# Output weights and input loads moved ahead on the DMA queues, and half-depth matmuls joined in bursts, in a fused convolution and mixing kernel

## The chip, the cores and the metric

One Trainium2 chip, one core. The metric is device time in microseconds (us), as the median of several executions. Names of the engines: PE is TensorE (matmul), PEld its weight load, DVE VectorE, ACT ScalarE, POOL GpSimd, SP SyncE. DMA has one queue for each of three kinds of traffic here: inputs are read by POOL's queue (q0 of the profile), outputs stored by SP's queue (q1), and q8 brings PE its instructions, which will matter.

Executions of a one-core kernel can be labelled slow only by their time (over 1.5% above the fastest of the same kernel). Where I meet that label below I say what was behind it, since here it was never the whole clock of a run.

## The reference, cut to what matters

```python
B, S, D = 8, 4224, 192                      # x, float32
# 1. causal depthwise convolution, 7 taps, softmaxed weights, 8 groups of 24 channels
out[b, s] = sum_k softmax(weight)[h, k] * x_pad[b, s + k]
# 2. linear attention form on that result
wq, wk = x @ w_q, x @ w_k                   # 192 -> 64
W_tok  = einsum('bsd,btd->bst', wq, wk) / sqrt(64)
mixed  = einsum('bst,btd->bsd', W_tok, x)
return maximum(mixed, 0) @ w_out            # 192 -> 192
```

The kernel never builds the 4224x4224 product: it forms G = x^T x per batch, M = w_k^T G, and then mixed = (x w_q) M.

## The kernel before: the parts that matter here

PE runs a fixed list of jobs, one letter each, and every engine does its work in the order that the list gives: Y (convolution as a banded matmul), G (six 64-column matmuls), Q (48 matmuls of 32x64 tiles), Z (one 512-column matmul; three of them give "mixed" for 1024 tokens, which lie in two halves of 64 rows; the first two each meet zeros in one half of the rows, the third serves both halves on a diagonal), O (output product of 512 tokens, two PSUM banks). Evacuations from PSUM go to ACT and DVE, also in order.

```python
    wload(WK[64:128, 2], wk_t, 0, DH, wl[1], 2)
    load(1, 0)                                   # loads of batch 1, all on POOL's queue
    load(1, 1)
    ...
    load(1, 2)
    ...                                          # zeros, identity
    load(1, 3)
    load(2, 0)
    wload(WO1[:, :], wo_t, 0, D, wl[2])          # the output weights
    wload(WO2S[0:64, :], wo_t, 128, D, wl[2])
    wload(WO2S[64:128, :], wo_t, 128, D, wl[2])
    z_wo2 = pool(lambda e: e.memset(WO2[:, :], 0.0))
    load(2, 1)
```

WO2 holds the last 64 rows of the output weights twice, on a diagonal of a zero-filled 128x384 tile, so that one full-depth matmul serves two blocks of tokens:

```python
            for j in range(2):                   # job O
                for h in range(2):
                    e.matmul(o[:, 192 * h : 192 * h + 192], z[:, h, cols], WO1[:, :],
                             start=h == 0, stop=False, **kw)
                last = e.matmul(o[:, 0:384], z[:, 2, cols], WO2[:, :], start=False, stop=True, **kw)
```

A store waits only for the evacuations that fill its buffer (`evs`):

```python
                st = P.dma("sp", lambda e, ...: e.dma_start(bass.AP(out_t, at, dims), src),
                           og[orr], evs)
```

The list was made with a model of the chip that also knows instruction fetch: `"fetch": (64, 256, 6.0, 3.0, 120.0)` says that PE's instructions come in blocks of 256, and that 6.0 us (3.0 after 120 us) have to lie between a block's start and the next one's.

Of the kernel before, what the change touches and what calls it, by code (L numbers as in the profile page):

```python
# [11 lines left out]


ORDER = (
    "YYDYYYDYDGDGGGYDGYYGDGTYTYDhYGhGTGDGGhGGHTGQYDGGWGTEMYMTYYYDZYZGGGTQYZGDGWGGDZZZ"
    "YOZOOGGGGhGGZTTHGYQGGGYYGYZDEZTYYZGZMGTGDTYGTYZTMGGGGOGOOGGHZQTGGYZGOYZOZZGYDZGY"
    "TGGZOZZOEYTTOGGYZGQGGYGTZDYZGHMhOGGZQYTGMTGYTTYOZOGOGZZGTZOYOOGZZOGZGDYGEQTGZZMG"
    "GhQOGZGYYTZOOGHGZYTOGGZMDYGGGYGZGYYOZGZGOZZGDGEOTZQGZMZGGTOYYOGTOZYGDYZZGGhMOGGT"
    "QHOGZGZTZOGZYOGGZZZYYZGOGYTTOTZOGZGhOEDQZGOYOGTGZTGGMYYOZOGGMZYZODGTOOGHZZGGYZOh"
    "GGGYThQGZZGZQZTOGYGEZYOOZZZOMYDGYMYGGZGTZOOTZZZGTGGTYDTGOGOGGQZZZGGOTTZTGZOQZGGO"  # L20
    "QGOGOEMZZZOMOOZZZOZZZZOOOZZZOOZZZOZOOOO"
)
# [3 lines left out]
    "x0": (5.0, 7.5, 9.0, 8.1, 10.2, 12.0, 13.1, 13.8), "band": 6.5, "wq": 14.0, "wk": 16.0,  # L26
    "wo": 26.0, "fill": 24.0,
    "dma": (377e3, 13.2, 1.6, {"x": 3.0, "o": 1.2}), "fetch": (64, 256, 6.0, 3.0, 120.0),
}
# [137 lines left out]
def bass_lightweight_conv__then__hypermixer_token_mlp_kernel(  # L167
# [8 lines left out]
    B, S, D = x.shape  # L176
# [16 lines left out]
    NZ = 3  # L193
# [76 lines left out]
    def rows(b, half, c, lo, hi, n, grp, deps):  # L270
        spent[0] += 0.45 + 0.055 * n
        at = (b * S + half * HALF + c * CW - 6 + lo) * D

        def f(e):
            return e.dma_start(  # L275
                XW[lo:hi, b % NX, half, c : c + n, :],
                bass.AP(x_t, at, [[D, hi - lo], [CW * D, n], [1, D]]),
            )

        return P.dma("pool", f, grp, deps)  # L280
# [62 lines left out]
    def wload(o, src, row0, width, grp, twice=1):  # L343
        spent[0] += 0.65
        n = o.shape[0]
        dims = [[width, n], [0, 2], [1, width]] if twice == 2 else [[width, n], [1, width]]
        P.dma("pool", lambda e: e.dma_start(o, bass.AP(src, row0 * width, dims)), grp)  # L347
# [104 lines left out]
    load(1, 0)  # L452
    load(1, 1)
    wq = [pool(lambda e: e.tensor_copy(WQ[:, :, :], WSQ[:, :, :]), [wl[0]], 0.55)]
    z_wk = pool(lambda e: e.memset(WK[:, 3:6], 0.0))
# [11 lines left out]
    load(2, 0)  # L467
    wload(WO1[:, :], wo_t, 0, D, wl[2])
    wload(WO2S[0:64, :], wo_t, 128, D, wl[2])
    wload(WO2S[64:128, :], wo_t, 128, D, wl[2])  # L470
    z_wo2 = pool(lambda e: e.memset(WO2[:, :], 0.0))
# [270 lines left out]
    def job_o(b, i, q):  # L742
# [19 lines left out]

        def make(bk):
            if rem:
                return [(OUT[:, orr, 0, 0:192], PS[:, bk, 0:192])]
            if tail:
                return [(
                    OUT[:, orr, q, :].rearrange("p (h r d) -> p r h d", h=2, r=2),
                    PS[:, bk : bk + 2, 0:384].rearrange("p r (h d) -> p r h d", h=2),
                )]  # L770
            return [(
                OUT[:, orr, :, 384 * q : 384 * q + 384].rearrange("p h (r d) -> p r h d", r=2),
                PS[:, bk : bk + 2, 0:384].rearrange("p r (h d) -> p r h d", h=2),
            )]
# [3 lines left out]
        def then():  # L778
            if not rem and q == 0 and not tail:
                return  # L780
            evs = [o for k in range(0 if not tail else q, q + 1) for o in made[("OUT", b, i, k)]]
            at = (b * S + 512 * i) * D
            if rem:
# [7 lines left out]
            for at, dims, src in parts:  # L791
                st = P.dma(
                    "sp",
                    lambda e, at=at, dims=dims, src=src: e.dma_start(bass.AP(out_t, at, dims), src),
                    og[orr], evs,
                )
# [3 lines left out]
            def landed(t, st=st):  # L800
# [3 lines left out]
                               (64 * 2 * D if rem else 128 * 4 * D if tail else 128 * 8 * D) * 4,  # L804
                               landed))
            flow()
# [42 lines left out]

    SWITCH = {("F", "Q"): 0.096, ("Q", "F"): 0.115}  # L850
    FILL, SEE = 0.231, 0.055
# [8 lines left out]
    for b in range(B):  # L860
        for g in range(len(GROUPS[b])):
            x_at[id(xg[b][g])] = CLOCK["x0"][g] if b == 0 else 999.0
    RATE, at0, DELAY, LAND = CLOCK["dma"]
    queue = {"x": [], "o": []}

    def flow():
        left = {k: [[t, n / RATE, f, LAND[k]] for t, n, f in v] for k, v in queue.items()}
        t = at0
        while any(left.values()):
            busy = [v for v in left.values() if v and v[0][0] <= t]  # L870
            nxt = min([v[0][0] for v in left.values() if v and v[0][0] > t] + [1e9])
            if not busy:
                t = nxt
                continue
            dt = min(min(v[0][1] for v in busy) * len(busy), nxt - t)
            t += dt
            for v in busy:
                v[0][1] -= dt / len(busy)
                if v[0][1] < 1e-9:
                    _, _, f, late = v.pop(0)  # L880
                    f(t + late)

    def land(b, part):
        def f(t):
            x_at[id(xg[b][part])] = t - 1.5 * (b == 1)
        return f

    def put(b, part, t):
        chunks = 18 * 128 if part == 0 else 16 * 128 + 2 * (6 + LAST)
        if b == 1:  # L890
            chunks = (9, 9, 8, 8)[part] * 128 + 2 * (6 + LAST) * (part == 2)
        queue["x"].append((t + DELAY, chunks * D * 4, land(b, part)))
        flow()
# [39 lines left out]

    def pick(n):
        if n == 4:
            if hold:
                return hold[0], max(banks[k][0] for k in hold)
            bk = min(range(4), key=lambda k: max(banks[j][0] for j in range(k, k + 4)))
            return bk, max(banks[k][0] for k in range(bk, bk + 4))
        if n == 1:  # L940
            bk = min((k for k in (6, 0, 1, 2, 3, 4, 5) if k not in hold),
                     key=lambda k: banks[k][0])
            return bk, banks[bk][0]
        bk = min((k for k in (0, 2, 4, 1, 3, 5) if k not in hold and k + 1 not in hold),
                 key=lambda k: max(banks[k][0], banks[k + 1][0]))
# [47 lines left out]
    def place(job, t):  # L993
# [8 lines left out]
        if job.pe:  # L1002
# [10 lines left out]
            late, code[:] = stall(job.words, pop.start, job.pe_us)  # L1013
            pop.end = free["pe"] = pop.start + job.pe_us + late
            total[0] += late
        elif kind == "GEV":
            pop = done[("G", job.name[1], NCK - 1)]
            deps += [pop] + [done[a_] for a_ in job.after if a_[1] >= 0 and a_[0] != "G"]
        else:
            pop = None  # L1020
            deps += [done[a_] for a_ in job.after if a_[1] >= 0]
        done[job.name] = pop
        emptied = []
        for make, key, n, what in job.evacs:
            pairs = make(bk)
            waits = [pop] if job.pe else list(deps)
# [39 lines left out]
            emptied.append(ev)  # L1066
        if job.pe:
            pop.name = job.name
        for k in held:
# [4 lines left out]
        if kind == "D" and job.name[1] > 1:  # L1074
            prefetch(job.name[1] + NX - 2, job.name[2])

    place(casts[0], CLOCK["x0"][1])
    head["W"] = 1
    for c in ORDER:
        if c == "h":  # L1080
            bk = pick(4)[0]
            hold[:] = range(bk, bk + 4)
            continue
        s = {"E": "GEV", "M": "MC"}.get(c, c)
# [37 lines left out]
```

## Time and profile before

| | before |
|---|---|
| device time, median (range) | 159.91 us (159.88 to 160.38) |
| span of the profiled execution | 158.0 us |
| first output matmul | 29.75 us |
| last input load landed | 122.83 us |
| PE's end, tail after it | 151.1 us, 6.9 us |

The lines behind these are in the prediction. One row that it did not read is on the same page, under the DMA queues (packets, MB, share of the 16 engines' span): PE's instruction stream, 19 blocks of 16 KB.

```profile
q8 instruction: 19, 0.31, 0.7%
```

### The profile page before, as it was taken

The page shows a single profiled execution, that of the slowest core. Times are in us where ns is not written, and L with a number is a line of the kernel's source. Part 1 is how long each engine was busy: PE and PEld are TensorE (multiplying, and loading weights), DVE is VectorE, ACT ScalarE, POOL GpSimd, SP SyncE. Part 2 cuts the span into 40 slices and gives each one's busy share as a digit, 9 for nine tenths or more (in the row PEclk, how much of TensorE's full clock was granted, in tenths as well). Part 3 has the DMA queues.
Part 4 walks back from the last instruction along what each step waited for, and adds up shares of the span by engine and source line. Part 5 has one row for each costly group of instructions (what it writes and reads, how often), then busy time and mean ns, then how long its engine had stood idle before and what let it go on. Part 6 is the DMA issues. An engine that isn't in the chain of part 4 may idle for free.

```text
span 158.0 us, 5584 instructions
## 1 busy us (share of the span) xinstructions
PE 142.7 (90%) x2428; PEld 102.2 (65%) x2428; DVE 117.8 (75%) x235; ACT 128.7 (81%) x216; POOL 59.8 (38%) x77
## 2 busy tenths in 40 slices
PE   6997759499999999999999999999999899999920
PEld 1476547374876777777776776777766677776710
DVE  6739678558889869967979988878678798677700
ACT  5566576698989999988997989999999698799940
POOL 7999899896906273301720200202020200000000
PEclk9999999999999999999999999999999999999995
DMA  3999999999999999999999999999998946279995
GB/s 105 261 193 183 192 191 190 192 191 290 193 193 323 337 276 234 207 339 327 267 318 256 323 269 262 323 287 308 310 349 214 358 168 242 74 306 374 353 372 189
DMA packets 48441, 40.83 MB, mean 258 GB/s; under 512 B 37281, under 2 KB 40481, under 8 KB 48417
## 3 DMA queue, kind: packets, MB, share of 16 engines
q0 software_dynamic: 36384, 13.35, 70.9%
q1 hardware_dynamic: 12032, 27.14, 48.0%
q8 instruction: 19, 0.31, 0.7%
q14 instruction: 6, 0.04, 0.1%
HBM read 27.86 MB, written 25.95 MB: 341 GB/s over the span
## 4 chain that ended last, share of the span: by engine, by line
PE 45%; DMA 34%; POOL 14%; issue 2%; ACT 1%; ACTq 0%; DVE 0%; POOLq 0%; DVEq 0%
DMA xw<-in_x_dram 29%; PE ps L758 8%; PE ps L639 8%; POOL xw L275 8%; PE ps L760 8%; PE ps L715 7%; PE ps L539 7%; PE ps L609 5%; DMA wo2s<-in_moe_w_out_dram 5%; POOL wk L347 2%; POOL xw L292 1%; POOL y L954 1%; ACT y L954 1%; ACT o_sb L954 1%; POOL m_sb L457 0%
## 5 line engine op out<-in xcount | busy, mean ns | idle before, releaser
L954 ACT COPY o_sb<-ps 128x768 f32<-128x768 f32 (+1 forms) x61 | 46.6, 781 | 4.4 <-PE ps L760 3.0
L954 ACT CAST y<-ps 128x864 bf16<-128x864 f32 (+6 forms) x49 | 39.9, 836 | 6.9 <-PE ps L505 3.5
L758 PE MATMUL ps<-wo,zt 128*128 128x192 bf16 x256 | 42.2, 247 | 2.1 <-DVE wo L954 2.0
L639 PEld LDWEIGHTS ps<-y 128*128 128x128 bf16 (+1 forms) x864 | 35.5, 98 | 12.5 <-issue 2.9
L760 PE MATMUL ps<-wo,zt 128*128 128x384 bf16 x128 | 41.7, 326 | 0.0
L639 PE MATMUL ps<-y 128*128 128x64 bf16 (+1 forms) x864 | 40.1, 193 | 0.5 <-DVE y L954 0.5
L954 POOL COPY y<-y 128x1152 bf16<-128x1152 bf16 x12 | 13.8, 1147 | 63.8 <-ACT y L954 51.2
L950 DVE STREAM_TRANSPOSE yb<-y 128x576 int32<-128x576 int32 x48 | 35.2, 757 | 0.1
L958 DVE TENSOR_SCALAR zt<-ps 128x512 bf16<-128x512 f32 x46 | 30.7, 683 | 5.1 <-PE ps L715 4.7
L758 PEld LDWEIGHTS ps<-wo,zt 128*128 128x128 bf16 x256 | 26.6, 114 | 12.0 <-ACT wo L954 2.2
L275 POOL DMA_DIRECT2D xw<-in_x_dram x35 | 32.5, 940 | 2.0 <-POOL xw L434 1.1
L715 PE MATMUL ps<-qt,m_sb 128*128 128x512 bf16 x96 | 31.6, 380 | 0.0
L957 ACT ACTIVATE zt<-ps 128x512 bf16<-128x512 f32 x50 | 29.1, 611 | 0.5 <-PE ps L715 0.3
L539 PE MATMUL ps<-xw,band 128*128 128x432 bf16 x96 | 24.4, 346 | 0.9 <-DMA xw<-in_x_dram 0.9
L954 DVE CAST y<-ps 128x864 bf16<-128x864 f32 (+2 forms) x19 | 19.4, 1022 | 4.5 <-PE ps L539 3.7
L954 DVE CAST qt<-ps 128x288 bf16<-128x288 f32 (+1 forms) x30 | 11.6, 424 | 9.0 <-PE ps L609 8.9
L954 ACT CAST qt<-ps 128x576 bf16<-128x576 f32 (+1 forms) x18 | 10.8, 610 | 5.9 <-PE ps L609 5.4
L609 PE MATMUL ps<-yb,wq 32*64 32x288 bf16 x768 | 15.2, 284 | 0.0
L760 PEld LDWEIGHTS ps<-wo,zt 128*128 128x128 bf16 x128 | 14.5, 114 | 0.0
L609 PEld LDWEIGHTS ps<-yb,wq 32*64 32x64 bf16 x768 | 10.5, 102 | 2.6 <-issue 0.7
L505 PE MATMUL ps<-xw,band 128*128 128x120 bf16 (+4 forms) x96 | 9.0, 233 | 2.6 <-DMA xw<-in_x_dram 1.6
L715 PEld LDWEIGHTS ps<-qt,m_sb 128*128 128x128 bf16 x96 | 8.6, 98 | 3.6 <-issue 0.7
(74 smaller groups left out, 96.7 us busy)
## 6 DMA issues: line engine op xcount, KB each, us to landing
out_dram<-o_sb SPq DMA_DIRECT2D x31, 768.0 KB, 7.4
xw<-in_x_dram POOLq DMA_DIRECT2D x14, 432.0 KB, 17.9
xw<-in_x_dram POOLq DMA_DIRECT2D x14, 384.0 KB, 26.0
o_sb<-in_x_dram SPq DMA_DIRECT2D x2, 480.0 KB, 4.4
out_dram<-o_sb SPq DMA_DIRECT2D x16, 48.0 KB, 5.5
out_dram<-o_sb SPq DMA_DIRECT2D x2, 384.0 KB, 3.8
xw<-in_x_dram POOLq DMA_DIRECT2D x2, 240.0 KB, 6.5
xw<-in_x_dram POOLq DMA_DIRECT2D x1, 288.0 KB, 6.9
```

The costliest lines, as they stand in the source:

```text
L275: return e.dma_start(XW[lo:hi, b % NX, half, c : c + n, :], bass.AP(x_t, at, [[D, hi - lo], [CW * D, n], [1, D]]),)
L505: last = e.matmul(PS[:, bk + j // per, at : at + w], BAND[:, h, :], XW[:, b % NX, half, c0:c1, GRP * h : GRP * h + GRP], start=True, stop= ...
L539: last = e.matmul(PS[:, k + j, 0 : 48 * n].rearrange("p (c h d) -> p h c d", h=2, d=GRP), BAND[:, h, :], rhs, start=True, stop=True,)
L609: last = e.matmul(PS[64 * h : 64 * h + 64, bk + i, 0:288], WQ[r, j, :], rhs, start=j == 0, stop=j == 5, skip_group_check=True)
L639: last = e.matmul(PS[:, 7, 64 * k : 64 * k + 64], y[:, 64 * k : 64 * k + 128], y[:, 64 * k : 64 * k + 64], start=c + h + k == 0, stop=c == ...
L715: return e.matmul(PS[:, bk, :], m[:, parts[k] : parts[k] + 128], q, start=True, stop=True)
L758: e.matmul(o[:, 192 * h : 192 * h + 192], z[:, h, cols], WO1[:, :], start=h == 0, stop=False, **kw)
L760: last = e.matmul(o[:, 0:384], z[:, 2, cols], WO2[:, :], start=False, stop=True, **kw)
L950: return e.transpose(o, i)
L954: return e.copy(o, i) if eng == "act" else e.tensor_copy(o, i)
L957: return e.activation(o, i, AF.Relu)
L958: return e.tensor_scalar(o, i, 0.0, None, op0=ALU.max)
```

## The change

Its intent: let reads go ahead of stores where PE will need the data, bring the output weights early, and stop spending PE time on the zero halves of the first two Z matmuls and of the 384-column output matmul. The whole job list was made anew with it. The core of it:

```diff
+GATES = {0: 8, 3: 9, 5: 10, 10: 12, 15: 14}       # store: the half batch whose load it waits for
 ORDER = (...)                                     # new list, with thirteen "A" = a burst
 CLOCK = {
-    "wo": 26.0, ... "fetch": (64, 256, 6.0, 3.0, 120.0),
+    "wo": 20.5, ... "fetch": (64, 256, 5.5, 3.5, 120.0),

     load(1, 0)
     load(1, 1)
+    wload(WO1[:, :], wo_t, 0, D, wl[2])
+    wload(WO2S[0:64, :], wo_t, 128, D, wl[2])
+    wload(WO2S[64:128, :], wo_t, 128, D, wl[2])
...
     load(1, 3)
     load(2, 0)
-    wload(WO1[:, :], wo_t, 0, D, wl[2])
-    wload(WO2S[0:64, :], wo_t, 128, D, wl[2])
-    wload(WO2S[64:128, :], wo_t, 128, D, wl[2])
     z_wo2 = pool(lambda e: e.memset(WO2[:, :], 0.0))   # stays here
     load(2, 1)

-                    og[orr], evs,
+                    og[orr], evs + wait,
...
+        def tails(e):                             # a burst: two Z, then the third-of-rows of O
+            for h in range(2):
+                rows = slice(64 * h, 64 * h + 64)
+                e.matmul(PS[:, za[h], :], M_SB[rows, ...], QT[rows, ...], start=True, stop=True)
+            for bk, z, cols in parts:
+                for r in range(2):
+                    for h in range(2):
+                        rows = slice(64 * h, 64 * h + 64)
+                        e.matmul(PS[:, bk + h, 192 * r : 192 * r + 192], z[rows, 2, cols[r]],
+                                 WO2S[rows, :], start=r == 0, stop=False)
+        def heads(e):                             # then the full-depth matmuls of the same O
+            ...
+                        e.matmul(PS[:, bk + h, 192 * r : 192 * r + 192], z[:, h, cols[r]],
+                                 WO1[:, :], start=False, stop=r == 1)
```

The planner's parts (how it models shares of the DMA engines, how banks are picked for a burst) changed too; they only produced the list and what is fixed with it, such as which bank and which evacuating engine a job gets.

## The prediction

> **What bounds the kernel now.** I read the page first, then the PE and POOL timelines of the start, the waits, the windows, and the DMA packets summed per queue. From the page:
>
> ```profile
> span 158.0 us, 5584 instructions
> PE 142.7 (90%) x2428; PEld 102.2 (65%) x2428; DVE 117.8 (75%) x235; ACT 128.7 (81%) x216; POOL 59.8 (38%) x77
> PE   6997759499999999999999999999999899999920
> DMA  3999999999999999999999999999998946279995
> q0 software_dynamic: 36384, 13.35, 70.9%
> q1 hardware_dynamic: 12032, 27.14, 48.0%
> ```
>
> PE is ragged for eight slices (31.6 us), full up to slice 30 (120 us), dented there, full until it ends. DMA is full up to 120 us, half idle for 20 us, full at the end. So three things set the time: a start in which PE waits, a long stretch of PE work, and a DMA tail. The 31.6 us of the start hold two waits that the PE timeline names:
>
> ```profile
> 20.12 0.90 PE L505 MATMUL ps<-xw,band 128*128 128x216 bf16 x8
> 22.61 0.53 PE L505 MATMUL ps<-xw,band 128*128 128x216 bf16 x4 [1.59 <-DMA xw<-in_x_dram]
> ...
> 27.23 0.53 PE L505 MATMUL ps<-xw,band 128*128 128x216 bf16 x4
> 29.75 0.33 PE L758 MATMUL ps<-wo,zt 128*128 128x192 bf16 x2 [1.99 <-DVE wo L954]
> 29.92 0.33 PE L760 MATMUL ps<-wo,zt 128*128 128x384 bf16 x1
> ```
>
> The output weights arrive last of all that the first output job (O) needs. POOL issues them late, behind batch 2's first load:
>
> ```profile
> 18.23 1.99 POOL L275 DMA_DIRECT2D xw<-in_x_dram  x2 [0.30 <-POOL xw L434]
> 20.20 0.57 POOL L347 DMA_DIRECT2D wo<-in_moe_w_out_dram  x1
> 20.75 1.10 POOL L347 DMA_DIRECT2D wo2s<-in_moe_w_out_dram  x2
> ```
>
> The later dent is one wait for the last input load (batch 7, second half), issued near 77 us and landed 46 us later, as the chain of waits shows:
>
> ```profile
> 77.17 45.66 DMA xw<-in_x_dram
> 122.83 0.14 issue
> 122.96 0.52 PE ps L539 x2
> ```
>
> The windows for 124 to 140 us show PE full and DMA at 0.55: PE has fallen behind and DMA has nothing to send.
>
> ```profile
> 124.00:140.00 16.00, 16.00 (x331) 11.92 (x328) 13.28 (x27) 14.22 (x24) 1.15 (x1) 1.00 0.55 206
> ```
>
> **What the Trainium skill says.** "DMA: Bandwidth & Descriptors", section "Queues, rings and completion order": each DMA engine takes turns between its queues, packet by packet. The trace agrees, and the turns are uneven in bytes. I counted packets in half-microsecond steps (input bytes doubled: the cast writes bf16 of float32): input alone moves about 376 GB/s; while a 768 KB store moves, input has 76 and the store 305. A store runs 2.6 us so and starts 3.4 us after its issue; the sum stays near 376 from 8 to 120 us.
>
> "TensorE: Matmul & The Clock Gate", "Part 3: Packing small matmuls — row/col tiling": matmuls on different row groups of the array run together. The trace agrees for 32x64 tiles: a Q job's 48 matmuls of 288 columns start 0.88 us before the next job, where one after the other they would take 5.9. No 64-row tile occurs in this trace. "TensorEngine Tiling (Array Packing)", "Key Properties", says that a change of mode drains the array. Here that costs some 0.24 us per Q job: 0.09 ahead of it, 0.15 in it beyond six times 0.1225.
>
> **The change part by part.** Start-to-start times of jobs in the trace are 0.655 us for O, 0.216 for a Z matmul, 0.175 for G (six 64-column matmuls), 0.366 for two 432-column Y matmuls. Summed over the job list they make 127.1 us, and 131.0 with 16 Q switches of 0.24. Up to the first O they make 14.0, so 117.0 remain. PE took 121.35 us for these (29.75 to 151.1): 4.35 us of stalls, of which 1.03 is the wait for batch 7. So 3.3 us are ordinary stalls, and I keep them.
>
> 1. Output weights earlier. The three issues (1.67 us of POOL) move ahead of the remaining loads of batch 1, to about 12.5 us. Loads land in order at full rate: batch 1's second load landed at 19.44, so the weights should land near 20 instead of 29.1. Batch 1's third load is pushed from 22.5 to about 23.0 (0.2 MB more ahead of it). The Q weights' cast goes from 12.4 to 14.1 and the identity from 16.2 to 17.8; the first Q (16.25 before) and the transpose (19.36) still come after. The new list puts 2 us more work before that third load's use, which covers the 1.59 us wait. Walking it: batch 0's last Y at 14.3 (its data at 13.36 is unchanged), nine G and a Q to 17.1, two Y and the transpose to 18.2, a wait to 19.45 for batch 1's second load, two Y, MM, Q and five Z to 22.6, a wait to 23.0, then five matmul jobs, Y and G, to 25.3. Evacuation of those Z, Q and Y tiles (7 us of ACT and DVE together in 3.5) may cost half a microsecond: first burst at 25.8. Work ahead of it is 12.8 + 0.5 = 13.3. The lag of the clock behind the work was 29.75 - 14.0 = 15.75 and becomes 12.5: **3.2 us gained**.
>
> 2. Bursts. Thirteen times, two Z (0.43) and one O (0.655), 1.087 together, become: two half-depth Z at once (0.216), four half-depth tail matmuls in two pairs (0.17), four heads (0.33), and two switches (about 0.21 to 0.24). That is 0.93 to 0.96; **1.9 us gained** in all, half of what it would be without switches. A burst needs two Z banks and two O banks free at once, so I take off 0.4 for the set. The O job's 128x384 matmul used half of its rows and columns on zeros, and two of three Z matmuls have zeros in one half: this is why no work is lost. Evacuations stay as many and as large.
>
> 3. Gated stores. The bytes stay; their order changes. Gates hold store 0 for batch 4's first half, 3 for its second, 5, 10 and 15 for the first halves of batches 5, 6 and 7. With the measured 376, 76 and 305 GB/s I moved both queues by hand along the new list: batch 3's halves land at 38 and 42 us (used 41 and 47), batch 4's at 47 and 51, store 0 leaves at 47 instead of 32.5; batch 5's at 65 and 69 (used 70 and 81), batch 6's at 82 and 87 (92 and 97), batch 7's at 100 and 105 (105 and 116). After each gate opens, the 3.4 us before the store moves are reads alone: 1.3 MB, most of a half batch of 1.6 MB. So **1.0 us gained**, the wait at 122 us. The same walk for the kernel before gave 121.7 for its last load (measured 122.83). Eight output buffers: the job that reuses store 10's buffer comes at 93, that store lands at 90; the others have 3 us or more. No new wait on this count, but the margin is small.
>
> Sum: 3.2 + 1.9 + 1.0 - 0.4 = 5.7, so PE ends at 145.4 instead of 151.1. From PE's end to the span's end were 6.9 us (last copy, stores queued at 366 GB/s); the last job is the same kind, and the last eight stores of 4.9 MB need 13 us in both lists, with 10.5 us of work from the first of them to the last against 9.7 before. I keep 6.9. Span 152.3, plus the 1.9 us between span and measured time: 154.2.
>
> **Rivals.**
> A. *DMA is the bound.* 52.4 MB at 376 GB/s are 139 us, plus 3 at the start and 2 to land: 145. For it: DMA full up to 120 us. Against: 9 us idle between 120 and 142, so earlier work fills that hole first; the total stays 7 us under my span. If stores held back come out in a heap at the end, 156.
> B. *The gates turn on the kernel.* The 3 us margins of output buffers fail, PE waits for copies that wait for stores near 77, 93 or 110 us. Each miss costs 1 to 3 us; two of them give 157 to 158.
> C. *64-row matmuls don't overlap.* A burst is then 1.09 + 0.2 of switches + nothing saved, the thirteen cost 2.6 instead of gaining 1.9: 158.5. For it: no such tile in the trace, and each 192-column pair needs two weight loads of 128 columns in 85 ns. Against: the Q job's overlap, and full-depth weight loads already keep up with one matmul per 29 ns in G.
> D. *Evacuation is the bound.* ACT was busy 109.4 of 120.5 us in the steady part, DVE 98.1: 91 and 81%. The steady part shortens by 2% only, so ordinary stalls may grow by a microsecond or two: 155.5.
> E. *The gates are needed more than I count.* The walk with the new list but no gates loses 4 us on batch 3, as store 0 would take bandwidth at 33 us. That says nothing against the sum, but an undo of the gates alone should show it.
>
> **Range and chances.** The start is good to about 1 us, the bursts to 1, the rest (B, D) leans late. 154.2 with 152.0 to 157.2. Two per cent faster is 156.7, which needs 3.2 of the 5.7 us: 0.87. Within two per cent, by C or two misses of B: 0.11. Slower: 0.02.
>
> **What would show it.** First output matmul near 25.8 us and no wait on the output weights; landings of these near 20; a burst's start-to-start near 0.94 with two half-depth matmuls starting together; no PE wait for input after 30 us; store 0 issued near 47; DMA share in 120 to 140 us well over 0.55; PE's end near 145.4 and 7 us of tail. Wrong if output copies wait for stores, if bursts exceed 1.09, or if the tail grows past 8 us.

## The result, and the profile after

| | before | predicted | after |
|---|---|---|---|
| device time, median | 160.14 (4 runs beside it) | 154.2 | **157.83** (4 runs, 157.18 to 158.32) |
| span, profiled execution | 158.0 | 152.3 | 156.2 |
| first output matmul | 29.75 | 25.8 | 27.22 |
| from there to PE's end | 121.35 | 119.6 | 122.8 |
| PE's end, tail | 151.1, 6.9 | 145.4, 6.9 | 150.0, 6.2 |

The ratio of after to before is 0.985 (95% interval 0.981 to 0.990). Ratios here are the mean time of one kernel's fast runs over that of the other's of the same rounds, so not quite the ratio of the medians. The change gained 2.3 us, where I had said 5.7 and given 0.87 to a gain of over two per cent; with a line drawn at two per cent, these runs count as the same. The three terms of the miss add up to the 3.9 us between the spans: the start is 1.4 late, the long stretch 3.2 longer, the tail 0.7 shorter.

The page of the changed kernel, cut to the lines that answer those of before:

```profile
span 156.2 us, 5628 instructions
PE 138.2 (88%) x2431; PEld 101.4 (65%) x2456; DVE 119.7 (77%) x239; ACT 128.7 (82%) x213; POOL 58.5 (37%) x76
...
PE   6989758989999899999999999999697999998940
...
DMA  3999999999999999999999999999997556599896
...
q8 instruction: 19, 0.31, 0.7%
```

PE's work did shrink, from 142.7 us busy to 138.2. But the share of PE in the span fell from 90 to 88%: PE now stands still in places where it did not before. The page shows one such place, the two digits 6 and 7 between 109 and 121 us, and the ragged start.

**The bursts work.** PE timeline, start, duration, job, and in brackets the idle time before it and who ended it:

```profile
26.57 0.69 PE L644 MATMUL ps<-y 128*128 128x64 bf16 x18
27.22 0.39 PE L1127 MATMUL ps<-qt,m_sb 64*128 64x512 bf16 x2
27.43 0.34 PE L1135 MATMUL ps<-wo2s,zt 64*128 64x192 bf16 x4
27.71 0.52 PE L1143 MATMUL ps<-wo,zt 128*128 128x192 bf16 x4
28.07 0.33 PE L763 MATMUL ps<-wo,zt 128*128 128x192 bf16 x2
```

Two 64-row matmuls of 512 columns (first burst line) take 0.39 us together, what one alone takes elsewhere on this timeline (0.38): they run at once. From the first burst line to the job behind it are 0.85 us; with the 0.10 of the switch ahead of it a burst costs 0.945 us against 1.087 for what it replaces.

**The start has a new wait.** PE, then ACT and POOL in the same stretch:

```profile
21.35 0.95 PE L614 MATMUL ps<-yb,wq 32*64 32x288 bf16 x48 [0.52 <-ACT y L975]
23.98 1.05 PE L720 MATMUL ps<-qt,m_sb 128*128 128x512 bf16 x4 [1.67 <-ACT m_sb L980]
```

```profile
20.33 0.88 ACT L975 CAST y<-ps 128x864 bf16<-128x864 f32 x1 [0.82 <-PE ps L510]
22.22 0.72 ACT L975 COPY wo<-wo2s 64x192 bf16<-64x192 bf16 x2 [1.01 <-POOL wo L476]
22.96 0.73 ACT L980 ACTIVATE m_sb<-ps 64x192 bf16<-64x192 f32 x3
```

```profile
19.70 2.04 POOL L280 DMA_DIRECT2D xw<-in_x_dram  x2 [0.30 <-POOL xw L439]
21.75 0.44 POOL L476 MEMSET wo<- 128x384 bf16 x1
```

The weights landed at 20.3 us at the latest, as predicted. But the zero fill of the tile they are copied into stayed behind batch 2's first load in POOL's order, and ends at 22.19. ACT takes its work in order: it stands for 1.01 us before the copies into that tile, and the copies of M, which PE's Z jobs need, stand behind these. PE waits 1.67 us.

**The long stretch has stops that no engine causes.** PE near 110 and 118 us:

```profile
109.38 0.33 PE L765 MATMUL ps<-wo,zt 128*128 128x384 bf16 x1
110.11 0.34 PE L544 MATMUL ps<-xw,band 128*128 128x432 bf16 x1 [0.41 <-DVE qt L975]
111.53 0.36 PE L544 MATMUL ps<-xw,band 128*128 128x432 bf16 x1 [1.07 <-issue]
111.72 0.38 PE L720 MATMUL ps<-qt,m_sb 128*128 128x512 bf16 x1
...
117.67 0.52 PE L1143 MATMUL ps<-wo,zt 128*128 128x192 bf16 x4
119.28 0.33 PE L763 MATMUL ps<-wo,zt 128*128 128x192 bf16 x2 [1.08 <-ACT o_sb L975]
```

The second and third line are two matmuls of one and the same job; no semaphore lies between them. The profile names "issue": PE waited for nothing that it shows. The stop at 118 is put down to ACT, but we shall see that it has the same cause. Smaller ones stand within a G job at 33 us (0.47 idle), behind a Q job at 54.66 (0.46) and inside a Q job near 61.5.

What do they have in common? I counted PE's instructions in the trace from the first one on: a weight load, its matmul and each wait count as one. The stops come at numbers 962, 1730, 1986, 3778 and 4034. All are 194 more than a multiple of 256. A block of q8 is 16,384 bytes, 256 instructions. So these are the edges between two blocks of PE's program. The trace has the time of each q8 packet; for the edges near the end of the stretch this gives (all in us, edges good to 0.1; "spare" is from the packet's end to PE's going over the next edge):

| kernel, execution | edge crossed | next block's packet | next edge crossed | spare |
|---|---|---|---|---|
| after | 103.44 | 109.10 to 110.05 | 111.54 | 1.49 |
| after | 111.54 | 116.80 to 117.68 | 119.12 | 1.44 |
| before | 100.25 | 102.71 to 103.64 | 107.41 | 3.77 |
| before | 107.41 | 109.81 to 110.73 | 114.30 | 3.57 |

Each trace has as many packets as edges (19 of each here), and up to 120 us each packet starts some microseconds after its edge, while the other queues move data: on average 3.0 us later in the kernel before (edges from 27 to 120 us, 3.65 at most), 4.15 us in the kernel after (5.66 at most). It takes 0.9 to 1.0 us. In all these traces PE never went over the next edge less than 1.25 us after a packet's end; so it needs each packet at the very next edge, and holds no more than the block that it runs and the one after it. In the kernel before, every packet came with at least 2.1 us to spare (edges from 27 us on, up to 122), so PE never stopped; in the kernel after five came too late (and a sixth, at 96.3, by a few tenths).

The Trainium skill has this mechanism ("Runtime: NRT & Kernel Launch", section "Instruction fetch mechanics"): the sequencer fetches its next 256 instructions through a DMA queue of its own while it works through the current ones, and the page calls the cost "mostly hidden". The packets and the spacing of the stops agree with the first half; "mostly hidden" holds for the kernel before and not for the one after.

**What was as predicted.** Store 0 was issued at 47.70 us (47 predicted). The halves of batch 3 landed at 38.6 and 43.0 (38, 42), batch 4 at 47.6 and 54.2 (47, 51), batch 5 at 65.8 and 70.1 (65, 69), batch 6 at 83.3 and 88.4 (82, 87), batch 7 at 101.6 and 105.9 (100, 105). PE waits for no input after 30 us. The windows for 120 to 136 and 124 to 140 us (length, busy time of PE, PEld, DVE, ACT, POOL, granted clock, DMA share, GB/s):

```profile
120.00:136.00 16.00, 15.74 (x305) 12.06 (x308) 12.71 (x25) 13.65 (x22) 1.15 (x1) 1.00 0.62 230
124.00:140.00 16.00, 15.74 (x276) 12.34 (x279) 13.14 (x29) 14.17 (x25) 0.00 (x0) 1.00 0.63 236
```

The idle hole of DMA filled less than I thought: the share in the second window rose from 0.55 to 0.63, which is not "well over". PE was 3 to 4 us later than predicted, so the work that fills the hole came later too.

### The profile page after: what moved, and what is told of

It reads as the page before. It is cut to its first block, busy times and chain, and to the rows that moved or that the text cites. A ratio compares the mean times of both kernels' runs of the same rounds, so it can differ in the third digit from the quotient of the medians.

```text
span 156.2 us, 5628 instructions
## 1 busy us (share of the span) xinstructions
PE 138.2 (88%) x2431; PEld 101.4 (65%) x2456; DVE 119.7 (77%) x239; ACT 128.7 (82%) x213; POOL 58.5 (37%) x76
## 3 DMA queue, kind: packets, MB, share of 16 engines
HBM read 27.86 MB, written 25.95 MB: 345 GB/s over the span
## 4 chain that ended last, share of the span: by engine, by line
PE 72%; POOL 13%; issue 5%; DVE 4%; ACT 2%; ACTq 0%; POOLq 0%
PE ps L644 15%; PE ps L544 12%; PE ps L763 11%; PE ps L765 9%; PE ps L614 8%; POOL xw L280 7%; PE ps L720 6%; PE ps L1143 3%; PE ps L1127 3%; POOL wk L352 1%; PE ps L1135 1%; ACT o_sb L975 1%; PE ps L510 1%; DVE zt L979 1%; POOL xw L297 1%
## 5 line engine op out<-in xcount | busy, mean ns | idle before, releaser
L975 ACT CAST y<-ps 128x864 bf16<-128x864 f32 (+6 forms) x47 | 38.2, 833 | 7.2 <-PE ps L510 3.6
L975 POOL COPY y<-y 128x1152 bf16<-128x1152 bf16 x11 | 12.6, 1146 | 62.4 <-ACT y L975 41.5
L979 DVE TENSOR_SCALAR zt<-ps 128x512 bf16<-128x512 f32 x44 | 29.4, 681 | 8.5 <-PE ps L720 3.9
L763 PE MATMUL ps<-wo,zt 128*128 128x192 bf16 x204 | 33.7, 247 | 1.9 <-ACT o_sb L975 1.2
L765 PE MATMUL ps<-wo,zt 128*128 128x384 bf16 x102 | 33.2, 326 | 0.0
L763 PEld LDWEIGHTS ps<-wo,zt 128*128 128x128 bf16 x204 | 21.2, 114 | 8.4 <-ACT o_sb L975 1.6
L975 DVE CAST y<-ps 128x864 bf16<-128x864 f32 (+2 forms) x21 | 21.6, 1026 | 4.1 <-PE ps L544 2.5
L720 PE MATMUL ps<-qt,m_sb 128*128 128x512 bf16 x45 | 15.3, 380 | 1.8 <-ACT m_sb L980 1.7
L975 ACT CAST qt<-ps 128x576 bf16<-128x576 f32 x16 | 10.3, 641 | 4.4 <-PE ps L614 3.7
L765 PEld LDWEIGHTS ps<-wo,zt 128*128 128x128 bf16 x102 | 11.6, 113 | 0.0
L544 PEld LDWEIGHTS ps<-xw,band 128*128 128x128 bf16 x96 | 7.4, 98 | 5.5 <-issue 1.3
```

Of the source, the lines that this page charges most:

```text
L544: last = e.matmul(PS[:, k + j, 0 : 48 * n].rearrange("p (c h d) -> p h c d", h=2, d=GRP), BAND[:, h, :], rhs, start=True, stop=True,)
L720: return e.matmul(PS[:, bk, :], m[:, parts[k] : parts[k] + 128], q, start=True, stop=True)
L975: return e.copy(o, i) if eng == "act" else e.tensor_copy(o, i)
L979: return e.tensor_scalar(o, i, 0.0, None, op0=ALU.max)
```

## The experiments

Theory after the first look: two things are missing from the gain, the late zero fill (over 1 us) and the fetch stops (3 to 4 us); the three parts of the change themselves are worth what I said. Rivals: R1, the gates hold stores back and this costs later (heaps of stores); R2, the bursts cost more than they show, by evacuations that bunch; R3, the early weights only exchange one wait for another. Twelve runs, in four groups; each group is compared with the kernel before on its own chip.

### e1_zero_early: the zero fill right behind the weight loads

```diff
     wload(WO2S[64:128, :], wo_t, 128, D, wl[2])
+    z_wo2 = pool(lambda e: e.memset(WO2[:, :], 0.0))
...
     load(2, 0)
-    z_wo2 = pool(lambda e: e.memset(WO2[:, :], 0.0))
     load(2, 1)
```

> The changed kernel with one POOL instruction moved: the zero fill of the block-diagonal output weights stands right behind their three loads instead of behind batch 2's first load. Theory: in the changed kernel ACT waits for this fill (idle to 22.2 us), does the two copies that need it, and only then copies the M tile that the first Z matmul waits for (1.67 us of PE). Moved, the fill is done near 15 us: no such wait, first burst at 25.8 instead of 27.2, time down 1.0 to 1.5 us (156.4 to 156.8 if the changed kernel is 157.8). Rival: the start is bound by evacuation of Z and Q tiles anyway; the first burst moves by less than 0.5 us and the time stays within 0.4 us of the changed kernel.

Measured: median 156.82 us of six, but in two groups: 153.72 and 154.01, and four from 156.73 to 158.23, which were labelled slow by their time. Their granted clock (0.989 to 0.995) is that of the others. The ratio of the fast runs is 0.963 (0.959 to 0.966). The profile is of an execution of the slow group:

```profile
22.76 1.04 PE L720 MATMUL ps<-qt,m_sb 128*128 128x512 bf16 x4 [0.69 <-ACT m_sb L980]
...
25.93 0.39 PE L1127 MATMUL ps<-qt,m_sb 64*128 64x512 bf16 x2
```

The wait for M fell from 1.67 to 0.69 us and the first burst came at 25.93, where I had predicted 25.8. That part of the theory stands. The same trace has stops of 1.98 us ahead of 110.23 (put down to "issue") and 1.65 ahead of 118.71 (put down to ACT), both at block edges, after packets that started 5.9 and 5.8 us late. Their sum, 3.6, is the distance between the groups (3 to 4 us).

### e2_no_gates: the five waits taken away, all else equal

```diff
-                    og[orr], evs + wait,
+                    og[orr], evs,
```

> The changed kernel with the five stores' waits for input loads taken out, everything else and every engine's order the same. Theory of the prediction (gates protect the reads): store 0 goes at 33 us, batch 3's halves land at 44 and 50 instead of 38.6 and 43, PE waits for them by 3 to 4 us; time 160.5 to 162. Rival (gates do harm: the held stores come out in a heap at 102 to 118 us, instruction fetches wait behind them for 5.3 us and more instead of 3 to 4, and PE stands at two instruction block edges for 1.2 us each): these two stalls shrink to under 0.4 each, which gives 2 us back; time 158.5 to 160 with the waits for batch 3 still there, and under 157.8 if those are smaller than I walk.

Measured: 160.35 us, ratio 1.003 (1.000 to 1.005). PE waits for batch 3 and later:

```profile
42.79 0.34 PE L644 MATMUL ps<-y 128*128 128x64 bf16 x6
44.94 0.52 PE L544 MATMUL ps<-xw,band 128*128 128x432 bf16 x2 [1.81 <-DVE xw L973]
...
51.18 0.52 PE L544 MATMUL ps<-xw,band 128*128 128x432 bf16 x2 [0.74 <-DMA xw<-in_x_dram]
```

```profile
100.71 0.52 PE L544 MATMUL ps<-xw,band 128*128 128x432 bf16 x2
102.57 0.54 PE L544 MATMUL ps<-xw,band 128*128 128x432 bf16 x2 [1.34 <-DMA xw<-in_x_dram]
```

That is 3.9 us of waits, near the 4 us that rival E of the prediction named. So the gates are needed by the new list, and R1 is no explanation: without them the kernel is 2.5 us slower than with them, not faster. Whether the gates lengthen the packets' lag this trace does not tell: the two large stops near 110 and 118 us are absent from it (lags of 3.8 and 2.4 us at the edges at 107.4 and 114.3), but at 49.8 us a packet came 5.2 us late without any gate.

### e3_no_bursts: each burst replaced by its two Z and one O in the list

```diff
 ORDER = (
-    ... "GZTYGGATZOYOHG" ...
+    ... "GZTYGGZZOTZOYOHG" ...          # each A becomes ZZO, thirteen times
```

> The changed kernel with each of the thirteen bursts written as its two Z jobs and one O job at full depth. Theory: a burst takes 0.945 us against 1.087, so PE's work grows by 1.85 us, less the 52 instructions that fall away (fetches come a little rarer): time 0.8 to 1.9 us above the changed kernel, 158.6 to 159.7. Rival (bursts need four free banks and two modes, and cost what they save): time within 0.5 us of the changed kernel, or below it.

Measured: 161.42 us, ratio 1.013 (1.009 to 1.017). That is 3.6 us over the changed kernel, twice the 1.85 us of the bursts, and some 6 us over its short group (see after_again), which is the fairer base, since this trace has no fetch stop over 0.2 us either. The profile shows PE waiting for evacuations, mostly ahead of Q jobs, where there was no such wait before the edit; two of the four places (the others: 0.70 at 52.95, 0.81 at 98.02):

```profile
109.75 0.25 PE L684 MATMUL ps<-gt,wk 128*128 128x64 bf16 x3
110.79 0.95 PE L614 MATMUL ps<-yb,wq 32*64 32x288 bf16 x48 [0.79 <-ACT y L975]
```

```profile
116.23 0.34 PE L644 MATMUL ps<-y 128*128 128x64 bf16 x6
117.95 0.95 PE L614 MATMUL ps<-yb,wq 32*64 32x288 bf16 x48 [1.39 <-ACT zt L978]
```

Together 3.7 us. The edit also lets the planner give banks and evacuating engines differently, so this run does not measure the bursts alone. It shows that they don't hurt (R2 falls) and that the list is tuned to them; their size rests on the 0.945 us on the timeline.

### e4_shift64: 64 more PE instructions ahead of everything

If the stops are block edges, they must move when the program moves. The kernel starts with matmuls that only warm PE up; six of 512 columns became 38 of 80. That is about as many columns (3040 for 3072), and 32 more weight loads and matmuls each.

```diff
-    def warm(n, deps):
+    def warm(n, deps, w=512):
...
-    warm(6, [])
+    warm(38, [], 80)
```

> The changed kernel with 64 more instructions on PE ahead of all work: the six warm-up matmuls of 512 columns become 38 of 80, in the same idle time. Work, order and waits are untouched. Theory (waits for nothing are instruction fetches at edges of blocks of 256): the stalls without a releaser again stand at instruction 194 modulo 256 counted from the start, so they move 32 matmuls ahead in the job list: none at the old places (inside batch 1's G job at 32.6 us, behind the Q job at 53.9, inside the Q job at 61, between two Y matmuls at 110.1). The time may go either way by up to 1.5 us. Rival (banks, evacuation, the queue of PE): the stalls stay at the same four jobs, time within 0.3 us.

Measured: 156.29 us of seven, ratio 0.978 (0.975 to 0.980). Nothing else in the program changed. The stops at 110 and 118 are gone, and there are new ones:

```profile
94.56 0.71 PE L544 MATMUL ps<-xw,band 128*128 128x432 bf16 x3
96.09 0.36 PE L544 MATMUL ps<-xw,band 128*128 128x432 bf16 x1 [0.82 <-issue]
...
102.62 0.43 PE L644 MATMUL ps<-y 128*128 128x64 bf16 x9
103.56 0.25 PE L644 MATMUL ps<-y 128*128 128x64 bf16 x3 [0.52 <-issue]
```

By count these are the instructions 3266 and 3522: 194 more than a multiple of 256 again. With that, the fetch is shown as the cause, and not the work at 110 and 118 us. The packet after the new edge at 96.1 was 5.2 us late, before the last gate opened; so the stores held at that gate are not needed for it. Two of the seven runs (158.0, the profiled one, and 159.06) were longer. In the profiled one the granted clock was 0.57 from 24 to 28 us, which is 1.7 us of PE time, right behind the wait for M.

### after_again: the changed kernel once more, on another chip

> The changed kernel as it is, six more runs. The kernel with the early zero fill had runs of 153.7 to 154.0 and of 156.7 to 158.2 at the same granted clock. If fetch waits are a matter of luck in each execution, the changed kernel shows such a spread too: most runs 157 to 158.3, some below 156. If it does not, its four first runs (157.2 to 158.3) stand for it.

Measured: 155.65, 157.94, 155.07, 157.62, 155.69, 158.55; median 156.65. The ratio of the fast runs, 0.970 (0.967 to 0.973), takes the three short ones alone, the others being labelled slow at an equal clock (0.979 to 0.995; the short ones 0.977 to 0.997). With the first four, the ten runs form two groups: three from 155.07 to 155.69, seven from 157.18 to 158.55. This time the profile is of the short group:

```profile
109.65 0.53 PE L544 MATMUL ps<-xw,band 128*128 128x432 bf16 x2 [0.41 <-DVE qt L975]
110.01 0.38 PE L720 MATMUL ps<-qt,m_sb 128*128 128x512 bf16 x1
...
115.96 0.52 PE L1143 MATMUL ps<-wo,zt 128*128 128x192 bf16 x4
116.53 0.33 PE L763 MATMUL ps<-wo,zt 128*128 128x192 bf16 x2
```

The same instructions as in the fence of the result above, and no stop in either place; the ACT that the profile blamed at 118 did its work behind the same jobs here and PE didn't wait for it. The two packets started 3.06 and 2.24 us after their edges instead of 5.66 and 5.26. The two blocks took 6.85 and 6.49 us instead of 8.10 and 7.58: 2.34 us, the distance between the groups. What decides in an execution whether these packets come early or late, I could not find; in both traces stores were moving there. From the first burst to PE's end this execution took 119.81 us, the one of the first profile 122.82.

### e5_zero_shift64: the zero fill and the shift together

The edits of e1 and e4.

> The changed kernel with both repairs: the zero fill early, and 64 instructions more ahead of the work. Theory: they are independent, the first gives 1.0 to 1.5 us at the start, the second moves the block edges away from the worst places (1.5 us in the runs so far): 154.5 to 155.3. Rival: what the start gives is lost at the block edges or in the wait for inputs: 156 or more.

Measured: 155.33 us, ratio 0.971 (0.967 to 0.975), six runs in one group from 154.72 to 156.82. Stops remain (0.64 ahead of 93.85 and 0.52 ahead of 101.32), so a shift of 64 trades places for others.

### e6_before_gates: the kernel before with the five waits alone

The diff's `GATES` and `evs + wait` put into the kernel before.

> The kernel before with the five waits of stores alone, nothing else. Theory of the prediction: batch 7's last load lands near 105 us instead of 122.8, the PE wait of 1.03 us at 122 is gone, nothing else changes: 158.6 to 159.2. Rival (a heap of held stores lengthens the lag from block edge to instruction fetch, 3.0 us on average in the kernel before, and PE stands at edges near 110 and 118): lag there over 5 us, new waits without a releaser of 0.5 us or more, time 159.5 to 161.

Measured: 160.43 us, ratio 1.000 (0.996 to 1.004). The wait for batch 7 at 122 us (0.87 us of idle PE in the kernel before) is gone from its trace, no fetch stop has come (lags of 3.0 us on average), and from the first output job to its end PE took 120.47 us, 0.88 less than before. But the median is the same. The profiled execution had a granted clock of 0.5 for 3.4 us from 9.7 us on (0.71 to 0.86 in windows of 4 us) and its first output job came at 30.87 instead of 29.75, which hides the gain in that run. Of the six runs, two (159.27 and 159.43) are shorter than all eleven of the kernel before on that chip (159.65 to 160.70), and four (160.24 to 160.90) are not; what these four lost I can't say without their traces. So the "1.0 us gained" of the prediction shows in the trace and in two runs, not in the median. For R1 this is another no: no cost of the waits shows.

### e7_before_wo_early: the kernel before with the weights (and the zero fill) early

```diff
     load(1, 1)
+    wload(WO1[:, :], wo_t, 0, D, wl[2])
+    wload(WO2S[0:64, :], wo_t, 128, D, wl[2])
+    wload(WO2S[64:128, :], wo_t, 128, D, wl[2])
+    z_wo2 = pool(lambda e: e.memset(WO2[:, :], 0.0))     # all four removed further down
```

> The kernel before with the three loads of the output weights, and their zero fill, moved to where the changed kernel has the loads. Theory: the 2.15 us wait for the weights at 27.5 is gone, but the reads of batch 7 land when the DMA queues let them, near 122 us, whatever PE does: the wait there grows from 1.0 to 2 to 3 us, and the time falls by less than 0.6 us: 159.2 to 159.9. Rival (PE's work sets the end): the full 2 us stay, 157.8.

Measured: 161.11 us, ratio 1.005 (1.002 to 1.007), with one run of 164.42 labelled slow (mean clock 0.967). The first output job starts at 27.95 instead of 29.75, and then:

```profile
56.53 0.95 PE L609 MATMUL ps<-yb,wq 32*64 32x288 bf16 x48
59.89 0.53 PE L539 MATMUL ps<-xw,band 128*128 128x432 bf16 x2 [2.41 <-DVE xw L952]
```

PE waits 2.41 us for batch 4's first half. R3 is right for the old list without gates: store 0 was issued at 30.77 us instead of 32.54, batch 4's first half landed at 59.54 instead of 51.79, and PE pays there more than the 1.8 us that it had won. So early weights without gates give nothing here, and neither does the new list without gates (e2). That early weights and gates would pay together in the old list is not shown: no run has just these two.

### e8_zero_no_gate15: e1 without the last of the five waits

After e1 I believed that store 15's wait (for batch 7) makes the heap of stores at 105 to 117 us and so the two large fetch stops. Then taking it away should give a single group near e1's short one.

```diff
-                    og[orr], evs + wait,
+                    og[orr], evs + wait * (n != 15),
```

> The changed kernel with the early zero fill and without the last of the five waits (store 15 for batch 7's first half). Theory: the two PE stops of 1.2 to 1.9 us near 108 and 116 us in the slower executions come from instruction fetches that lag 5 to 6 us behind the block edge while held stores alone fill the DMA queues. Without this gate no such heap: lag at both edges under 4 us, no group of runs 3 us above the fastest. In exchange batch 7's first half lands near 108 instead of 103 and PE waits 1 to 2 us for it. Runs within 1.5 us of each other, median 154.5 to 156. Rival (the spread has another cause): two groups again, 3 us apart, both some 1.5 us later than those of the early zero fill.

Measured: 161.46 us, ratio 1.004 (1.000 to 1.007). That theory fell. The profile is of the longest run, 164.52 us, which was labelled slow:

```profile
104.99 0.69 PE L644 MATMUL ps<-y 128*128 128x64 bf16 x18
113.37 0.90 PE L544 MATMUL ps<-xw,band 128*128 128x432 bf16 x2 [7.69 <-DVE xw L973]
```

Batch 7's first half landed at 113.1 us instead of 101.6, and PE stood for 7.7 us (the granted clock was 0.5 from 109.2 to 119.4 us, so over part of the wait and 6 us of work behind it). I had expected a wait of 1 to 2 us. The fast runs, 159.92 to 161.7, suggest that a wait of several microseconds is usual; only the slow one has a trace. Taking this one gate away costs as much as taking all five (e2). And although the gate was gone, the packet after the edge at 101.75 was 5.5 us late, so the stores that it holds are not what makes such a lag.

### e9_zero_shift32 and e9_zero_shift96: the zero fill and other shifts

32 and 96 more instructions ahead, again with about as many columns in all (96 also takes the first four warm-up matmuls: 20 of 102 columns).

```diff
+    z_wo2 = pool(lambda e: e.memset(WO2[:, :], 0.0))     # as in e1
-    warm(6, [])
+    warm(22, [], 140)                                    # e9_zero_shift32
```

> Early zero fill, and 32 instructions more ahead of the work (22 warm-up matmuls of 140 columns for six of 512). Theory: PE's stops without a releaser stand at instruction 194 modulo 256 again, so 16 matmuls earlier in the job list than in the changed kernel; how long they are depends on what the block before holds. 153.5 to 157; with 64 more the median was 155.3. Rival: no dependence on the alignment, the two groups at 154 and 157.5 as with the early fill alone.

> Early zero fill, and 96 instructions more ahead of the work (20 and 38 narrow warm-up matmuls for four and six wide ones). As with 32: stops at instruction 194 modulo 256, 48 matmuls earlier in the job list than in the changed kernel; 153.5 to 157. Rival: as with 32.

Measured, shift 32: **153.88 us**, ratio 0.961 (0.958 to 0.965), five of six from 153.36 to 154.18, one 155.39. Shift 96: 156.28 us of five, ratio 0.974 (0.973 to 0.976), with stops of 0.75 us ahead of 22.73, 1.21 ahead of 65.25 and 0.55 ahead of 114.49. The page and PE's timeline of shift 32:

```profile
span 151.7 us, 5660 instructions
PE 138.2 (91%) x2447; PEld 103.0 (68%) x2472; DVE 119.3 (79%) x237; ACT 128.8 (85%) x215; POOL 58.7 (39%) x76
```

```profile
22.83 1.04 PE L720 MATMUL ps<-qt,m_sb 128*128 128x512 bf16 x4 [0.69 <-ACT m_sb L980]
...
26.02 0.39 PE L1127 MATMUL ps<-qt,m_sb 64*128 64x512 bf16 x2
```

```profile
92.55 0.33 PE L763 MATMUL ps<-wo,zt 128*128 128x192 bf16 x2
93.84 0.35 PE L765 MATMUL ps<-wo,zt 128*128 128x384 bf16 x1 [0.96 <-issue]
```

PE is as busy as in the changed kernel (138.2 us), but the span is 4.5 us shorter. One large stop is left, and the edges at 100.8 and 106.7 are crossed 2.2 and 1.7 us after their packets. PE ends at 145.77 us, where the prediction had 145.4. This version beats both kernels. DMA's share from 124 to 140 us, by the way, is now what the prediction meant by "well over 0.55":

```profile
124.00:140.00 16.00, 15.38 (x256) 11.71 (x258) 12.61 (x26) 14.33 (x24) 0.00 (x0) 1.00 0.81 304
```

### e10_shift32: the shift without the zero fill

```diff
-    warm(6, [])
+    warm(22, [], 140)
```

> The changed kernel with 32 instructions more ahead of the work and the zero fill left late: what the alignment alone is worth. With both the median was 153.9. If the two repairs add, the late zero fill costs 1.0 to 1.6 us here as elsewhere: 154.9 to 155.5, one group of runs, and the wait of 1.67 us for the M tile is back near 22 us. If the alignment gave all of it: 153.9 to 154.3.

Measured: 156.17 us, ratio 0.973 (0.970 to 0.977): 154.97 and 154.99, and four from 155.96 to 156.42. The zero fill seems worth 2.3 us on top of this shift, more than the 1.3 by which it moved the first burst. The profile, of a run of 156.42, shows why: PE waits for M as in the changed kernel, and behind that wait the clock drops (column before the DMA share).

```profile
24.00:28.00 4.00, 4.00 (x30) 2.67 (x28) 2.93 (x5) 2.72 (x6) 3.65 (x6) 0.57 1.58 186
28.00:32.00 4.00, 4.00 (x62) 3.24 (x60) 3.29 (x6) 3.98 (x7) 3.54 (x6) 1.00 1.61 193
```

The same eight 216-column matmuls took 1.65 us in this dip and 0.91 in e9_zero_shift32, and the first burst came at 28.67 instead of 26.02. Clock 0.57 for 4 us is 1.7 us of work. From the first burst to its end PE took 119.71 us here and 119.75 there: so the difference lies in the start. The shortest run of this kernel against the shortest of e9_zero_shift32 gives 154.97 - 153.36 = 1.6 us, and e1's short group against the changed kernel's gives the same (155.07 - 153.72 = 1.35; 155.69 - 154.01 = 1.68). So I estimate the zero fill at 1.4 to 1.7 us, and in some runs another microsecond by the clock. Why the clock drops there in some executions and not in others is open; the changed kernel's first profile has the same wait and a clock of 1.00.

### All runs side by side

| kernel | median us | ratio to before |
|---|---|---|
| before (five sets) | 159.75 to 160.41 | 1 |
| changed, first four runs | 157.83 | 0.985 |
| after_again: short group | 155.65 | 0.970 |
| e1_zero_early: short group | 153.87 | 0.963 |
| e2_no_gates | 160.35 | 1.003 |
| e3_no_bursts | 161.42 | 1.013 |
| e4_shift64 | 156.29 | 0.978 |
| e5_zero_shift64 | 155.33 | 0.971 |
| e6_before_gates | 160.43 | 1.000 |
| e7_before_wo_early | 161.11 | 1.005 |
| e8_zero_no_gate15 | 161.46 | 1.004 |
| e9_zero_shift32 | 153.88 | 0.961 |
| e9_zero_shift96 | 156.28 | 0.974 |
| e10_shift32 | 156.17 | 0.973 |

## Why the prediction was right or wrong, point by point

**The base of the sum: wrong, and this is the larger miss (3.2 us).** "So 3.3 us are ordinary stalls, and I keep them." The kernel after has new ones of another kind. PE's program comes in blocks of 256 instructions, and a block can follow the one before it only after the packet's lag, its own 0.9 to 1.0 us, and 1.3 us or more. At the five stops of the changed kernel the blocks were 6.7 to 8.1 us apart. The change made PE's work denser (fewer us for as many instructions) and packets later. Shown: e4 moved the stops by moving the program alone, after_again lost the two large ones without any edit when the packets were early, and from first burst to PE's end e9_zero_shift32, with the edges elsewhere, took 119.75 us and after_again, the same kernel, 119.81, where the prediction had 119.6 and the first profile 122.8. That they meet it so closely is in part luck: both still have a stop of a few tenths to 1 us. Two signs were there to be read: the row q8 on the page, and the diff itself, which lowers the planner's fetch interval from 6.0 to 5.5 us (and raises the one after 120 us from 3.0 to 3.5). The new list was made to a limit that the chip didn't keep.

**Step 1, weights: right in the landing, wrong in what follows (1.4 us of miss).** The weights landed near 20 us as said. "First burst at 25.8" was 27.22. I had moved the three loads in my walk, and counted as its cost only the evacuations of Z, Q and Y; that the zero fill stays behind batch 2's load, that ACT takes the weights' copies in order, and that M stands behind them, was left out. With the zero fill moved as well the first burst came at 25.93 and 26.02. The step's gain of 3.2 us was sized for a kernel that moves four operations, and this one moves three.

**Step 2, bursts: right.** "0.93 to 0.96" per burst was 0.945, "1.9 us" was 13 times 0.142, 1.85. The 0.4 us that I took off for banks is about right too: in after_again two of the thirteen bursts took 1.06 us from first line to next job instead of 0.85 and one started 0.15 late, together 0.57. The size is read from the timeline; e3 does not measure it.

**Step 3, gates: right in the landings (within 1.6 us, but for batch 4's second half at 54.2 for 51); the term's size stays open.** "1.0 us gained" was read as the wait removed at 122 us, which the timeline has at 0.87. In the old list the trace of e6 shows 0.88 us, but its median shows none; the new list loses 2.5 us without the gates (e2), and the early weights lose their 1.8 us in the old list without them (e7). So the three gains cannot be measured one at a time and added.

**The tail:** 6.9 predicted, 6.2 measured, 6.0 in e9_zero_shift32.

**The rivals.** A, DMA as the bound: no; DMA still idles over a third of 124 to 140 us. (Its 52.4 MB are 53.8 by the page, 27.86 read and 25.95 written, so 148 us and not 145.) B, output buffers: no wait of a copy for a store was seen. C: false, 64-row matmuls overlap. (By its own terms it would have been 154.2 + 1.9 + 2.6, 158.7; and in step 2 the 1.9 us are two fifths, not half, of the 13 times 0.371 that there would be without switches.) D, evacuation: it costs little in the changed kernel (0.41 us is the longest wait for a copy after 30 us that is not a fetch stop) and 3.7 us in e3, where the list no longer fits. E: about right, 3.9 us of waits against "4 us", though not all on batch 3. None of the five was what happened. The sixth, that PE may run out of instructions, was not on my list.

**The numbers together.** The bursts and the landings were right, and with the zero fill moved and the edges shifted the kernel comes to 153.88, near the 154.2 of the prediction. That is in part luck: a stop of 0.96 us is still in it, and a tail 0.9 us shorter than predicted makes up for it. As it was written, it gives 157.18 to 158.55 in most executions and 155.07 to 155.69 in some.

**What stays open:** why the lag of a fetch packet is about 3.0 us in all kernels with the old list and 3.4 to 4.3 in those with the new one, with gates and without; what decides between the two groups; why the gates alone gain nothing in four of six runs; how much of the gain is the new list's own, since no run has that list with the other parts taken out at once; what starts the dips of the clock.

## What to carry to other kernels

When a wait is removed by moving a load, follow everything else that the waiting operation needs, and every engine that takes its work in order, through to the next job: what stays behind becomes the wait. When gaps within PE are put down to "issue" in the middle of a job, count instructions: if they fall on the same remainder of 256, the program is waiting for its own text, and a few dozen instructions more or less ahead of it move the stops. Try several: here shifts of 32, 64 and 96 gave, with the zero fill early, 153.88, 155.33 and 156.28 us. And parts of a change that use the same bandwidth are to be valued together: the early weights gave nothing in a kernel without the gates.

## What the Trainium skill lacked or had wrong

- "Runtime: NRT & Kernel Launch", section "Instruction fetch mechanics", calls the cost of a block edge mostly hidden, since instructions are issued more slowly than they are fetched. On a PE that starts 256 instructions every 6 to 8 us, with the DMA engines full, it wasn't: the packet started 2.2 to 5.9 us after the edge in the long stretch of the changed kernel and its e1 variant, took 0.9 to 1.0 us, PE went over the next edge no sooner than 1.25 us after its end, and stops of 0.4 to 2.0 us followed. The page gives no such times, and no way to see these stops in a profile ("issue", or put down to an engine that had long been done).
- "TensorEngine Tiling (Array Packing)", section "Key Properties", says that a change of mode drains the array and gives no cost. Here a switch to 64-row tiles and back costs about 0.23 us, an estimate: a burst of 0.945 us holds 0.216 + 0.17 + 0.33 us of matmuls.
- No page says that the value of reads ahead of stores is not local: without one of five gates a load of 1.6 MB landed at 113.1 us instead of 101.6, and the kernel took 161.46 us instead of 153.7 to 158.
